# Batch 1's attention in 256-token blocks behind w2, and a re-ordered down projection, in a fused retention and mixer kernel

## The chip, the cores and the metric

The kernel runs on one core of one Trainium2 chip. The metric is the device time of one execution in microseconds, and the median over several runs is what counts. A core has five engines, each with its own in-order instruction queue: TensorE (PE; PEld is its weight load) multiplies matrices into PSUM banks, VectorE (DVE) and ScalarE (ACT) read those banks and write SBUF, GpSimd (POOL) works on SBUF alone, and SyncE (SP) issues transfers. ACT's queue issues transfers too.

## The reference, cut to what matters

Inputs q, k and v have the shape [4 batches, 8 heads, 768 tokens, 64]. The first half is a retention layer, the second a mixer with a low-rank mix over tokens and an MLP over channels:

```
for t in range(S):
    state = gamma * state + outer(k[t], v[t])      # per batch and head
    y[t] = (q[t] @ state) / sqrt(64)
x = y as [4, 768, 512]
u = x + (x^T @ U @ V)^T                            # U: 768 x 32, V: 32 x 768
out = u + relu(u @ w_ch1) @ w_ch2                  # 512 x 2048 and 2048 x 512
```

## The kernel before, in words

**The retention** is computed in pieces of tokens. Powers of gamma are multiplied into q and k when they are cast to bf16. For each piece, scores `a` are the product of k and q, masked (VectorE, L355 or L435); the output is `a` times v plus q times the running state (TensorE, L372/379 or L445/450), copied from PSUM to `xs[b]` by ScalarE; and the state is added up in one PSUM bank over the whole batch (L328 or L415) and copied out by ScalarE.

Batch 0 goes in three blocks of 256 tokens (`prep_block`, `turn_block`, `state_half`, `score_block`, `mix_block`). A partition of a block holds two successive tokens, so a load reads 512 bytes in a row. A block's score has two halves, each of 16 matmuls on a 64x64 part of the array. Batches 1 to 3 go in six chunks of 128 tokens, one token a partition, loads of 256 bytes in a row (`prep_chunk`, `turn_pe` or `turn_dma`, `state`, `score`, `mix`). q and k are needed transposed: batch 1 does that on TensorE (`turn_pe`, through PSUM bank 6 named "qk", evacuated by ScalarE), batches 2 and 3 by DMA transposes on ScalarE's queue.

**The low-rank mix** of a batch: `lr_proj` (L468), `lr_expand` (L478 and the adds at L482), and a transpose of the result into `uT`, by `lr_turn_pe` or by DMA (`lr_turn`).

**The MLP** has an up projection, 32 pieces (16 of 512 tokens, 16 of 256 tokens; four matmuls each, L624), whose ReLU goes to VectorE for each third piece (L629) and to ScalarE for the others (L631). Batch 0's down projection is 24 pieces of four matmuls (L659). The down projections of batches 1 to 3 use Strassen's scheme in Winograd's form: seven products p1 to p7 of half-size blocks for each of three pairs of token tiles, 21 pieces of eight matmuls (`down_pairs`, L552). It needs sums of blocks of w2 (`w2_sums`, 16 VectorE operations in four calls, made once) and of the hidden layer (`g_sums`, four calls of four VectorE operations in each batch). Products gather in PSUM banks named A, B and C; `keep` (L565) and `give` (L571) read them on VectorE.

**The order.** `weave` writes out all queues by hand: the MLP's pieces of batch b-1 in order, and between them the steps of batch b's attention and low-rank mix, each at a mark that is a share of the stage's summed piece costs (a full up piece counts 0.864, a down piece 0.864 or 0.874). A step is put before the first piece that begins at or after its mark.

**Loads.** One list, `feed`, holds all loads in order; SP issues them. Sixteen are issued ahead, and each `take` of a loaded tile issues one more, since a tile's buffer has to be read before it is filled again. The order is batch 0, U and V, w1, one chunk of batch 1 (`AHEAD`), w2, the rest of batch 1, U again in another layout, batches 2 and 3. GpSimd casts nearly everything that is loaded, in the order of the list. The rows of `out` are stored when both halves of a row are ready: batch 0 by SP, in two halves for its interleaved token order, batches 1 to 3 by ScalarE's queue.

**PSUM** has eight banks, given out in rings by `RINGS` (L68): "mlp" has banks 0 to 2, "s" 3 and 4, "o" 5, "qk" 6, "st" 7, A takes 0 and 6 in turn, B 1, C 2.

Of the kernel before, what the change touches and what calls it, by code (L numbers as in the profile page):

```python
# [18 lines left out]
def kernel(  # L19
# [26 lines left out]
    AHEAD = 1  # L46
# [22 lines left out]
             "A": [0, 6], "B": [1], "C": [2]}  # L69
# [42 lines left out]
    def feed_block(sc):  # L112
        for nm, src in (("k", k), ("q", q), ("v", v)):
            for hh in range(2):
                feed.append(((nm, 0, sc, hh),
                             src[0, ds(4 * hh, 4), ts(sc, SC), :].rearrange(
                                 "h (p two) d -> p h (two d)", two=2)))
# [30 lines left out]
    for sc in range(NSC):  # L148
        feed_block(sc)
# [4 lines left out]
    for ci in range(AHEAD):  # L154
        feed_chunk(1, ci)
    for m in range(NM):
        feed.append((("w2", m), moe_w_ch2[ts(m, P)]))
    for b in range(1, B):
        for ci in range(NCK):
            if b > 1 or ci >= AHEAD:  # L160
                feed_chunk(b, ci)
        if b == 1:
            feed.append((("u2",), None))
# [71 lines left out]
    def prep_block(eng, nm, sc, hh):  # L235
        if hh == 0:
            pre[nm, sc] = blk.tile([P, 2, H, D], bf16, tag=nm + "0",
                                name=f"{nm}0_{sc}")
        t = pre[nm, sc][:, :, ds(4 * hh, 4)]
        src = take(nm, 0, sc, hh).rearrange("p (h two d) -> p two h d", h=4,  # L240
# [57 lines left out]
    def turn_block(nm, sc, eng):  # L298
        src = pre[nm, sc]
        tp = bank("mlp", bf16)  # L300
        t = blk.tile([P, 4, 2, P], bf16, tag=nm + "T0",
                      name=f"{nm}T0_{sc}")
# [12 lines left out]
        live[nm, sc] = t  # L315

    def state_half(sc, x):

        kd, vb = pre["k", sc], pre["v", sc]
        first = sc == 0 and x == 0  # L320
        if first:
            live["st_p"] = bank("st")
            live["st", 0, 0] = None
# [13 lines left out]
        live["st", sc + x, 1 - x] = ns  # L337

    def score_block(sc, par, tag="s", engs="DD"):
        kT, qT = live["k", sc], live["q", sc]  # L340
# [9 lines left out]
        for i in range(2):  # L350
            a = blk.tile([P, 4, P], bf16, tag=f"a0{i}{par}",
                          name=f"a0{i}{par}_{sc}")
# [8 lines left out]
            live["a", sc, par, i] = a  # L361

    def mix_block(sc, engs):
        if sc == 0:
            xs[0] = xp.tile([P, NCK, DM], fp16, tag="x", name="x_0")
        qT, vb = live.pop(("q", sc)), pre["v", sc]
        o_p = [bank("o"), bank("qk")]
        for x in range(2):
            st = live.pop(("st", sc, x))
            if st is not None:  # L370
                for p in range(4):
                    nc.tensor.matmul(o_p[x][:, ts(p, P)], qT[:, p, x], st[:, p],  # L372
                                     start=(p == 0), stop=False,
                                     skip_group_check=True)
        for par in range(2):
            for h in range(H):
                for x in range(2):
# [3 lines left out]
                        live["a", sc, par, h % 2][r, h // 2], vb[r, par, h],  # L381
                        start=(sc == 0 and x == 0 and par == 0 and h == 0),
                        stop=True, skip_group_check=True)
        for x in range(2):
            evac(engs[x], xs[0][:, 2 * sc + x], o_p[x])

    def turn_pe(b, ci, eng="A"):
        qkd, vb = pre[b, ci]  # L390
        tp = bank("qk", bf16)
        qkT = rmid.tile([P, 8, P], bf16, tag="qkT", name=f"qkT_{b}_{ci}")
        for i in range(2):
            for p in range(4):
                nc.tensor.transpose(tp[:, ts(4 * i + p, P)],
                                    qkd[:, i, ds(2 * p, 2)], ident)
        evac(eng, qkT, tp.rearrange("p (n m) -> p n m", n=8))
        live[b, ci] = [vb, qkT]

    def turn_dma(b, ci):  # L400
        qkd, vb = pre[b, ci]
        qkT = rmid.tile([P, 8, P], bf16, tag="qkT", name=f"qkT_{b}_{ci}")
        nc.scalar.dma_start_transpose(
# [22 lines left out]
    def score(b, ci):  # L426
# [6 lines left out]
        for i in range(2):  # L433
            a = rmid.tile([P, 4, P], bf16, tag=f"a{i}", name=f"a{i}_{b}_{ci}")
# [29 lines left out]
    def lr_proj(b):  # L464
        p_p = bank("o")
        for j in range(NCK):
            for c in range(NCB):
                nc.tensor.matmul(p_p[ds(RK * c, RK), :P], Ub[b > 0][:, j],  # L468
# [5 lines left out]
    def lr_expand(b, j0, nj, last="qk"):  # L474
        banks = [bank(t) for t in ("s", "s", "o", last)]
        for j in range(j0, j0 + nj):
            for c in range(NCB):
                nc.tensor.matmul(banks[c][:, ts(j - j0, P)],  # L478
                                 V4[b > 0][ds(RK * c, RK), ts(j, P)],
# [6 lines left out]
    def lr_turn_pe(b, j0):  # L486
        tp = bank("qk", fp16)
# [7 lines left out]
    def lr_turn(b, j):  # L495
        nc.scalar.dma_start_transpose(
# [11 lines left out]
    def store():  # L508
        if stores:
            eng, dst, src = stores.pop(0)  # L510
            eng.dma_start(out=dst, in_=src)

# [16 lines left out]
    def g_sums(gT, gS, m):  # L529
# [5 lines left out]
        nc.vector.tensor_tensor(s1, a21, a22, op=ALU.add)  # L535
        nc.vector.tensor_tensor(s2, s1, a11, op=ALU.subtract)
        nc.vector.tensor_tensor(a21, a11, a21, op=ALU.subtract)
        nc.vector.tensor_tensor(s4, a12, s2, op=ALU.subtract)

    def down_pairs(b, gT, gS):  # L540
# [21 lines left out]
        def keep(key, i, nm, j, h):  # L562
            t = outp.tile([P, DQ], fp32, tag=f"d{nm}", bufs=1,
# [5 lines left out]
        def give(key, i, j, h, more):  # L569
# [4 lines left out]
            if r[1] == 2:  # L574
                stores.append((nc.scalar, out[b, ts(j, P)], r[0]))
# [12 lines left out]

        def p5(i):
            product("C", i, s1, t1, True)  # L590

        def p7(i):
            product("A", i, s3, t3, False)
            keep("A", i, "c", i + NP, 1)
            give("C", i, i + NP, 1, held["c", i])
# [9 lines left out]
        order = []  # L605
        for i in range(NP):
            order += [(p1, i)] if i == 0 else []
            order += [(p2, i), (p6, i), (p5, i), (p7, i)]
            order += [(p1, i + 1)] if i + 1 < NP else []
            order += [(p4, i), (p3, i)]  # L610
        return [(0.874, part(f, i)) for f, i in order]

    def mlp_pieces(b):
# [4 lines left out]
        def up(m, lo, sz):  # L618
            j, nj = lo // P, sz // P

            def f():
# [6 lines left out]
                if n[0] % 3 == 0:  # L628
# [10 lines left out]
        else:  # L639
            def both(t, i):  # L640
                return [t[i], t[i + 1], t[i + NH], t[i + NH + 1]]

            pieces += both(lo, 0) + both(lo, 2) + both(hi, 0)
            pieces += both(hi, 2) + both(lo, 4) + both(hi, 4)
            pieces += both(lo, 6) + both(hi, 6)
            gS = gtp.tile([P, 3, NH, TH], fp16, tag="gS", name=f"gS_{b}")
            for i, at in ((0, 15), (2, 19), (4, 26), (6, len(pieces) - 1)):
                cost, f = pieces[at]
                pieces[at] = (cost, chain(f, part(g_sums, gT, gS, i)))
            return pieces + down_pairs(b, gT, gS)  # L650
        hold = {}

        def down(j, m0):
            def f():
# [6 lines left out]
                if m0 == NM - 4:  # L661
# [3 lines left out]
                    dst = out[b, ts(j, P)]  # L665
                    if b:
                        stores.append((nc.scalar, dst, o_sb))
                    else:
                        for i in range(2):
                            stores.append((nc.sync, dst.rearrange(  # L670
                                "(p two) c -> two p c", two=2)[i],
                                o_sb[ds(HP * i, HP)]))
# [37 lines left out]
    def prep_pair(nm, sc, engs):  # L710
        for hh in range(2):
            prep_block(engs[hh], nm, sc, hh)
# [3 lines left out]
    for sc in range(NSC):  # L716
        last = sc + 1 == NSC
        keep_busy(3 if sc else 9, fresh=True)
        turn_block("k", sc, "D")
        keep_busy(0 if sc else 7)  # L720
        turn_block("q", sc, "AD" if last else "A")
        prep_pair("v", sc, "PA")
        if sc:
            state_half(sc - 1, 1)
            mix_block(sc - 1, "AA")
        else:
            keep_busy(4)
        score_block(sc, 0)
        if not last:
            prep_pair("k", sc + 1, "PD")  # L730
            keep_busy(3)
            score_block(sc, 1)
            prep_pair("q", sc + 1, "PD")
            keep_busy(1)
        else:
            score_block(sc, 1, "mlp", "DA")
        state_half(sc, 0)
# [5 lines left out]
    mix_block(NSC - 1, "AD")  # L743
# [20 lines left out]

    for ci in range(AHEAD):
        prep_chunk(1, ci)
    for j in range(4):
        prep_w2(j)
    for b in range(1, B + 1):
        tracks = []  # L770
        if b > 1:
            first = [part(lr_expand, b - 1, 4, 2),
                     part(lr_turn_pe if b == 2 else lr_turn, b - 1, 4)]
        tracks.append((first, 0.02, 0.2 if b == 1 else 0.06))
        if b < B:
            if b == 1:
                at = [0.5, 0.6, 0.655, 0.715, 0.77, 0.825]
                lag = [0.01, 0.035, 0.065]
                turn = turn_pe
                for i in range(AHEAD, NCK):  # L780
# [54 lines left out]
```

## Time and profile before

| | us |
|---|---|
| median of 13 runs | 247.17 (244.94 to 249.11) |
| the profiled execution's own time | 245.95 |
| its span, from the first to the last instruction | 244.1 |
| TensorE busy | 217.5 |
| VectorE busy | 145.8 |
| ScalarE busy | 87.5 |
| GpSimd busy | 83.9 |

A few groups of instructions from the page's table. The columns are the line, the engine, the operation, what is written from what, the tiles and the count; then the busy time and the mean nanoseconds of one; then the idle time of the engine just before, and what ended it:

```profile
L624 PE MATMUL mlp<-uT,w1b 128*128 128x512 f16 (+1 forms) x512 | 89.3, 326 | 3.4 <-ACT gT L631 1.3
...
L435 DVE TENSOR_TENSOR a<-s,mask 128x512 bf16<-128x512 f32 x36 | 23.0, 680 | 7.5 <-PE s L431 7.5
...
L552 PE MATMUL A<-w2t,gS 128*128 128x256 f16 x72 | 9.3, 272 | 4.1 <-DVE da L565 4.1
```

The up projection is the largest group. TensorE sat idle for little of the time before any one group; a wait for VectorE's `da` is the largest of the down products. The duration that a timeline row shows for a group of matmuls ends after the next group has begun, because matmuls are pipelined; the step from start to start is what a group costs the queue.

### The profile page before, as it was taken

How to read it: one execution, taken by the hardware profiler on the slowest of the kernel's cores; microseconds unless marked ns; L12 is line 12 of the kernel's file. 1: busy time of each engine (PE TensorE's matmuls, PEld its weight loads, DVE VectorE, ACT ScalarE, POOL GpSimd, SP SyncE). 2: the span in 40 equal slices, each digit the busy share in tenths (PEclk: the TensorE clock that was granted, in tenths of full speed). 3: DMA queues.
4: the chain of work that ended last, by engine and by line, in shares of the span. 5: the costliest groups of instructions: out<-in, count | busy, mean ns of one | idle time of the engine just before them, and what ended most of it. 6: DMA issues, size and time to landing. Idle time of an engine off the chain costs nothing. (4 is left out here: it accounts for less than half of the span.)

```text
span 244.1 us, 5336 instructions
## 1 busy us (share of the span) xinstructions
PE 217.5 (89%) x2152; PEld 143.9 (59%) x2152; DVE 145.8 (60%) x289; ACT 87.5 (36%) x175; POOL 83.9 (34%) x121
## 2 busy tenths in 40 slices
PE   7898999999999589877679979999799889998993
PEld 3466544866555245543578753765688645656882
DVE  6577445338796632786575663496855652856442
ACT  3267354554643154554320002665221014541000
POOL 5542988687888481366425100000000000000000
PEclk9999999999999999999999999999999999999999
DMA  6998999999999998999993155322222352000222
GB/s 182 295 290 211 298 343 272 383 238 212 224 212 217 232 233 193 227 192 230 206 202 110 66 107 148 70 47 43 43 53 82 109 149 46 0 0 4 86 86 89
DMA packets 94633, 39.22 MB, mean 161 GB/s; under 512 B 78096, under 2 KB 87312, under 8 KB 94608
## 3 DMA queue, kind: packets, MB, share of 16 engines
q1 hardware_dynamic: 73008, 29.43, 51.9%
q10 hardware_dynamic: 21600, 9.44, 17.0%
q8 instruction: 17, 0.28, 0.5%
q14 instruction: 8, 0.07, 0.1%
HBM read 27.85 MB, written 6.29 MB: 140 GB/s over the span
## 5 line engine op out<-in xcount | busy, mean ns | idle before, releaser
L624 PE MATMUL mlp<-uT,w1b 128*128 128x512 f16 (+1 forms) x512 | 89.3, 326 | 3.4 <-ACT gT L631 1.3
L624 PEld LDWEIGHTS <-w1b 128*128 128x128 f16 x512 | 48.1, 98 | 35.7 <-issue 4.6
L631 ACT ACTIVATE gT<-mlp 128x512 f16<-128x512 f32 (+1 forms) x88 | 43.2, 498 | 62.9 <-PE mlp L624 39.7
L629 DVE TENSOR_SCALAR gT<-mlp 128x256 f16<-128x256 f32 (+1 forms) x40 | 21.4, 535 | 36.4 <-PE mlp L624 36.3
L552 PEld LDWEIGHTS <-gT 128*128 128x128 f16 x288 | 27.4, 98 | 8.0 <-issue 4.6
L435 DVE TENSOR_TENSOR a<-s,mask 128x512 bf16<-128x512 f32 x36 | 23.0, 680 | 7.5 <-PE s L431 7.5
L84 ACT ACTIVATE x<-o 128x512 f16<-128x512 f32 x21 | 12.5, 596 | 37.0 <-PE o L450 23.9
L552 PEld LDWEIGHTS <-gS 128*128 128x128 f16 x216 | 20.7, 98 | 7.2 <-issue 4.4
L659 PE MATMUL mlp<-w2b,gT 128*128 128x512 f16 x96 | 24.2, 380 | 0.0
L263 POOL TENSOR_TENSOR qkd<-in,gq 128x512 bf16<-128x512 f32 x18 | 19.4, 1076 | 10.7 <-DMA in<-in_q_dram 9.0
L263 POOL TENSOR_TENSOR qkd<-in,gk 128x512 bf16<-128x512 f32 x18 | 20.0, 1110 | 8.5 <-DMA in<-in_k_dram 8.3
L552 PE MATMUL A<-w2t,gT 128*128 128x256 f16 x144 | 18.6, 272 | 3.0 <-DVE dc L565 1.5
L84 ACT ACTIVATE state<-st 64x256 bf16<-64x256 f32 x40 | 15.0, 375 | 7.0 <-PE st L328 3.8
L261 POOL CAST vd<-in 128x512 bf16<-128x512 f32 x18 | 11.8, 654 | 15.8 <-issue 9.6
L552 PE MATMUL A<-w2t,gS 128*128 128x256 f16 x72 | 9.3, 272 | 4.1 <-DVE da L565 4.1
L450 PE MATMUL o<-vd,a 128*128 128x64 bf16 x144 | 8.0, 194 | 5.2 <-DVE a L435 5.0
L659 PEld LDWEIGHTS <-gT 128*128 128x128 f16 x96 | 8.2, 98 | 7.2
L177 PE MATMUL mlp<-ones 128*128 128x512 bf16 x34 | 10.9, 451 | 1.4 <-DVE ones L170 1.4
L482 DVE TENSOR_TENSOR x<-s,x 128x256 f16<-128x256 f32 (+1 forms) x16 | 8.2, 552 | 5.8 <-PE qk L478 4.7
L565 DVE TENSOR_TENSOR dc<-A,x 128x256 f32<-128x256 f32 x9 | 3.8, 424 | 11.9 <-PE A L552 11.9
L290 POOL CAST w2b<-in 128x512 f16<-128x512 f32 x16 | 9.8, 616 | 3.1 <-DMA in<-in_moe_w_ch_dram 2.4
L450 PEld LDWEIGHTS <-a 128*128 128x128 bf16 x144 | 6.2, 98 | 6.9 <-DVE a L435 6.4
(110 smaller groups left out, 271.8 us busy)
## 6 DMA issues: line engine op xcount, KB each, us to landing
in<-in_moe_w_ch_dram SPq DMA_DIRECT2D x32, 256.0 KB, 5.9
in<-in_k_dram SPq DMA_DIRECT2D x24, 256.0 KB, 5.2
in<-in_q_dram SPq DMA_DIRECT2D x24, 256.0 KB, 5.5
in<-in_v_dram SPq DMA_DIRECT2D x24, 256.0 KB, 5.4
out_dram<-o ACTq DMA_DIRECT2D x18, 256.0 KB, 2.0
out_dram<-o SPq DMA_DIRECT2D x12, 128.0 KB, 3.6
Vf<-in_moe_V_dram SPq DMA_DIRECT2D x4, 96.0 KB, 3.6
qkT<-qkd ACTq DMA_TRANSPOSE x12, 3.3
```

The costliest lines, as they stand in the source:

```text
L84: nc.scalar.activation(dst, src, AF.Copy)
L177: nc.tensor.matmul(idle_bank[0], ones[:, :P], ones, start=True, stop=True, skip_group_check=True)
L261: nc.gpsimd.tensor_copy(out=t, in_=src)
L263: nc.gpsimd.tensor_tensor(t, src, g[:, ci, :, None].to_broadcast([P, H, D]), op=ALU.mult)
L290: nc.gpsimd.tensor_copy(out=w2b[:, m], in_=take("w2", m))
L435: nc.vector.tensor_tensor(a, four(sp[i]), causal(mask), op=ALU.mult)
L450: nc.tensor.matmul(o_p[:, ts(h, D)], a[i][:, h // 2], vb[:, h], start=(ci == 0 and h == 0), stop=True, skip_group_check=True)
L552: nc.tensor.matmul(acc[key, i], lhs[:, m, ts(i, P)], rhs[:, m], start=(fresh and m == 0), stop=(m == NH - 1), skip_group_check=True)
L624: nc.tensor.matmul(g_p[:, :sz], w1b[:, c, ts(m, P)], uTs[b][:, ds(j, nj), c], start=(c == 0), stop=(c == NCB - 1))
L629: nc.vector.tensor_relu(gT[:, m, ds(lo, sz)], g_p[:, :sz])
L631: nc.scalar.activation(gT[:, m, ds(lo, sz)], g_p[:, :sz], AF.Relu)
L659: nc.tensor.matmul(ch, gT[:, m, ts(j, P)], w2b[:, m], start=(m == 0), stop=(m == NM - 1))
```

## The change

1. **Batch 1 in blocks.** It takes batch 0's path: three blocks, two tokens a partition, 512-byte loads. All its casts are on GpSimd. The k transpose is evacuated by ScalarE, the q transpose by VectorE; both use the "qk" bank, as does the second output of `mix_block`. Its token order is then interleaved, so it uses the first layout of U and V (`Ub[b > 1]`), and its rows of `out` are stored in two halves, on ScalarE's queue (`keep_row`).
2. **Its place.** No chunk of batch 1 is loaded ahead of w2 any more. The marks of its steps and of `w2_sums` are new.
3. **Down projection.** The 21 products come in a written-out order in which the A chains of pairs 0 and 1 interleave (two A banks, the first one 6); `give` of C's first result (`c22`) happens when both p5 and p7 are done; the `keep` tiles get two buffers.
4. **Spread sums.** The four operations of a `g_sums` call follow four successive pieces, one each; the last call's are put behind the last up piece (two) and the first two down pieces.
5. **Smaller edits.** From batch 1's MLP on, each fourth ReLU instead of each third goes to VectorE, and the "mlp" ring has four banks (6, 0, 1, 2). `lr_turn_pe` of batch 1's last part uses the "o" bank, `lr_expand` of the last tiles "st". The score tiles `a0` and `a1` have two buffers instead of four. Stores of batches 2 and 3 and the DMA transposes of batch 3 go to SP's queue.

The diff's core:

```diff
-    AHEAD = 1
-             "A": [0, 6], "B": [1], "C": [2]}
+             "A": [6, 0], "B": [1], "C": [2]}
...
-    for ci in range(AHEAD):
-        feed_chunk(1, ci)
     for m in range(NM):
         feed.append((("w2", m), moe_w_ch2[ts(m, P)]))
-    for b in range(1, B):
+    for sc in range(NSC):
+        feed_block(1, sc)
+    feed.append((("u2",), None))
+    for b in range(2, B):
         for ci in range(NCK):
-            if b > 1 or ci >= AHEAD:
-                feed_chunk(b, ci)
-        if b == 1:
-            feed.append((("u2",), None))
+            feed_chunk(b, ci)
...
+            pool, tag = (rpre, "qkd") if b else (blk, nm + "0")
...
+        tp = bank("qk" if b else "mlp", bf16)
...
-        nc.scalar.dma_start_transpose(
+        (nc.sync if b > 2 else nc.scalar).dma_start_transpose(
...
+            a = rmid.tile([P, 4, P], bf16, tag=f"a{i}", bufs=2,
...
+    def keep_row(b, j, row):
+        dst = out[b, ts(j, P)]
+        if b > 1:
+            stores.append((nc.sync, dst, row))
+            return
+        for i in range(2):
+            stores.append((nc.scalar if b else nc.sync, dst.rearrange(
+                "(p two) c -> two p c", two=2)[i], row[ds(HP * i, HP)]))
...
+        def c22(i, nm):
+            done.add((nm, i))
+            if ("p5", i) in done and ("p7", i) in done:
+                give("C", i, i + NP, 1, held["c", i])
...
-        order = []
-        for i in range(NP):
-            order += [(p1, i)] if i == 0 else []
-            order += [(p2, i), (p6, i), (p5, i), (p7, i)]
-            order += [(p1, i + 1)] if i + 1 < NP else []
-            order += [(p4, i), (p3, i)]
+        order = [(p1, 0), (p1, 1), (p2, 0), (p6, 0), (p6, 1), (p5, 0), (p7, 0),
+                 (p7, 1), (p2, 1), (p4, 0), (p3, 0), (p4, 1), (p5, 1), (p1, 2),
+                 (p2, 2), (p6, 2), (p3, 1), (p7, 2), (p5, 2), (p4, 2), (p3, 2)]
...
-                if n[0] % 3 == 0:
+                if n[0] % (3 if b == 0 else 4) == 0:
...
-            for i, at in ((0, 15), (2, 19), (4, 26), (6, len(pieces) - 1)):
-                cost, f = pieces[at]
-                pieces[at] = (cost, chain(f, part(g_sums, gT, gS, i)))
-            return pieces + down_pairs(b, gT, gS)
+            late(pieces, 12, g_sums(gT, gS, 0))
+            late(pieces, 16, g_sums(gT, gS, 2))
+            late(pieces, 24, g_sums(gT, gS, 4))
+            s1, s2, s3, s4 = g_sums(gT, gS, 6)
+            late(pieces, len(pieces) - 1, [chain(s1, s2)])
+            down = down_pairs(b, gT, gS)
+            late(down, 0, [s3, s4])
+            return pieces + down
...
-            first = [part(lr_expand, b - 1, 4, 2),
-                     part(lr_turn_pe if b == 2 else lr_turn, b - 1, 4)]
+            first = [part(lr_expand, b - 1, 4, 2, "st"),
+                     part(lr_turn_pe, 1, 4, "o") if b == 2 else
+                     part(lr_turn, b - 1, 4)]
+            if b == 2:
+                RINGS["mlp"] = [6, 0, 1, 2]
...
-                at = [0.5, 0.6, 0.655, 0.715, 0.77, 0.825]
-                lag = [0.01, 0.035, 0.065]
+                at = [0.46, 0.57, 0.68]
+                lag = [0, 0, 0.12]
+                for i in range(NSC):
+                    for nm, d in (("k", 0), ("q", 0.005), ("v", 0.01)):
+                        tracks.append((
+                            [part(prep_block, "P", nm, 1, i, hh)
+                             for hh in range(2)], at[i] - 0.1 + d, at[i] - 0.1 + d))
+                    for f, d in ((part(turn_block, "k", 1, i, "A"), 0),
+                                 (part(turn_block, "q", 1, i, "D"), 0.022),
+                                 (part(state_half, 1, i, 0), 0.03),
+                                 (part(score_block, 1, i, 0), 0.046),
+                                 (part(score_block, 1, i, 1), 0.07),
+                                 (part(mix_block, 1, i, "AA"), lag[2])):
+                        tracks.append(([f], at[i] + d, at[i] + d))
+                    if i + 1 < NSC:
+                        tracks.append(([part(state_half, 1, i, 1)],
+                                       at[i] + 0.085, at[i] + 0.085))
...
-                    tracks.append(([part(w2_sums, m)], 0.58 + 0.05 * m, 1))
+                    tracks.append(([part(w2_sums, m)], 0.46 + 0.025 * m, 1))
```

## The prediction

> **What bounds the kernel now.** I read the page's busy row first, then TensorE's waits, then the timelines of TensorE, VectorE and GpSimd around each gap.
>
> ```profile
> PE 217.5 (89%) x2152; PEld 143.9 (59%) x2152; DVE 145.8 (60%) x289; ACT 87.5 (36%) x175; POOL 83.9 (34%) x121
> ```
>
> TensorE (PE) is busy 217.5 of 244.1 us and runs one hand-ordered queue to the last product, so time is won or lost where that queue has work or waits. The clock row is 9 (full) in all slices. TensorE's timeline gives the stages: batch 0's attention to 28.6 us; batch 0's MLP with batch 1's attention woven in, 28.6 to 87.4 (stage 1); MLP 1 with batch 2's attention to 146.6 (stage 2); MLP 2 with batch 3's to 198.0 (stage 3); MLP 3 alone to the end (stage 4). What TensorE waited for:
>
> ```profile
> PE o L450 <- DVE a L435: 5.0, 7, 2.6
> PE A L552 <- DVE da L565: 4.1, 3, 2.0
> PE A L552 <- DVE dc L565: 1.5, 3, 0.5
> PE A L552 <- DVE db L565: 1.5, 2, 0.9
> ...
> PE qk L490 <- DVE x L482: 1.4, 2, 0.8
> ...
> PE s L478 <- DVE pc L86: 1.2, 1, 1.2
> PE qk L490 <- ACT uT L84: 1.1, 1, 1.1
> ```
>
> Nearly all are VectorE (DVE) late with a small tile behind a row of sums, none a load. By stage the timeline's gaps add to 4.0 us (stage 1 from 49.4 on), 10.0 (stage 2), 3.7 (stage 3), 2.2 (stage 4). The largest in stages 2 to 4:
>
> ```profile
> 108.03 0.29 PE L450 MATMUL o<-vd,a 128*128 128x64 bf16 x4 [1.01 <-DVE a L435]
> ...
> 116.90 0.29 PE L450 MATMUL o<-vd,a 128*128 128x64 bf16 x4 [2.58 <-DVE a L435]
> ...
> 123.39 1.03 PE L552 MATMUL A<-w2t,gS 128*128 128x256 f16 x8 [2.00 <-DVE da L565]
> ...
> 146.62 1.02 PE L624 MATMUL mlp<-uT,w1b 128*128 128x512 f16 x4 [0.54 <-DVE o L571]
> ```
>
> **Part 1: spread sums, new order of the down products, fourth MLP bank.** The p6-after-p1 gaps (2.00, 1.41, 0.65) arise because four sums of 0.55 us stand before `da`; now `da` stands behind two, and two products lie between: gone. The p4-after-p7 gaps (0.51 in each stage) get a product in between. The waits for a bank or evacuation (0.83, 0.50, 0.24, 0.47) go with four MLP banks and a free first A bank. But part of the gaps at the ends of stages 2 and 3 won't return. There the low-rank expansion starts at 138.55, its four adds end at 141.9, two DMA transposes are issued at 141.98 and 143.3, and a transpose takes 3.2 us to land: 146.5, just when the first product of MLP 2 starts. The new order leaves the same six products (5.2 us) after the expansion, so 0.94+0.51+0.54 in stage 2 and 0.57+0.51+0.53 in stage 3 stay as a wait for `uT`.
>
> Stage 4 gains 0.24+0.47+0.65+0.51 = 1.9; stage 3 gains 0.50+0.15+1.41 = 2.1. In stage 2 the 0.83, the 2.00 and the `a` waits (1.01+0.31+2.58+0.31) are open, 7.0 together; but VectorE still does 16 sums, now one per piece. At four half-size pieces of 0.44 us each with a sum of 0.57 (0.73 with GpSimd beside it) it falls behind, and masks queue there: I work out about 1 to 2.2 us left before the second `mix` and 1.1 to 1.7 before the fourth. Gain 3.0 to 6.0, taken 4.3. Sum of part 1: -8.3.
>
> **Part 2: batch 1 in blocks: TensorE's work.** From batch 0's rows (start to start): a state half 0.55 (8 products), a score half 0.35 (16), a block's mix 0.57, four state products 0.22, a block transpose 0.45. New: 5x0.55 + 6x0.35 + 3x0.57 + 5x0.22 = 7.7. Old: 5x0.22 + 6x0.33 + 6x0.23 + 5x0.22 = 5.6. Transposes: 48 either way. So +2.1, on the path, since TensorE hardly waits there. Evacuations are equal in number; three of six transposed tiles move from ACT to DVE (0.68 as batch 0's kT).
>
> **Part 3: batch 1 loaded behind w2.** GpSimd's casts show when loads came:
>
> ```profile
> 36.65 0.62 POOL L284 CAST w1b<-in 128x512 f16<-128x512 f32 x1 [0.22 <-DMA in<-in_moe_w_ch_dram]
> ...
> 52.67 0.62 POOL L290 CAST w2b<-in 128x512 f16<-128x512 f32 x1 [0.16 <-DMA in<-in_moe_w_ch_dram]
> 53.59 1.04 POOL L263 TENSOR_TENSOR qkd<-in,gq 128x512 bf16<-128x512 f32 x1 [0.31 <-DMA in<-in_q_dram]
> ```
>
> w1's last block landed at 36.6, w2's at 52.6, with three 256-byte-run loads between. Without those, w2's sixteen loads at 0.67 us (w1's best) to 0.82 end at 47.4 to 49.7. Then k's halves land 0.9 apart, as batch 0's, and cost GpSimd 1.04 each, then q's, then v's 0.61: k ready at 50.5 to 52.7, q 2.1 later, v 1.3 after that. TensorE reaches the first transpose (mark 0.46, before the 14th half-size piece) at 49.4; today's first chunk was prepared at 40. Wait 1.0 to 4.5 over k, q and v; taken 2.9. SP's later loads are queued behind the same ring as before; nothing else waits.
>
> [...]
>
> **Part 4: batch 1's chain of waits.** Blocks share bank 6 ("qk") between transposes and the second mix output; each next user waits for ScalarE (1.02 a transpose, 1.1 two x tiles). Walking the marks piece by piece (0.87 a full piece), waits appear: score half 2 behind the masks 0.6; first mix behind kT's evacuation 1.25; second q transpose 0.4; second mix 0.2; third q transpose, put right behind that mix, 1.25; projection behind two evacuations 0.4; the uT transpose one piece after the expansion instead of two, with its adds done 3.0 after it, 1.8, then 0.35. That is 6.25 without the w2 sums.
>
> The w2 sums move from every 0.1 of the stage to every 0.05, from mark 0.46. Their price now:
>
> ```profile
> 56.69 0.42 DVE L527 TENSOR_TENSOR w2t<-w2b,w2t 128x512 f16<-128x512 f16 x1
> 57.04 1.26 DVE L527 TENSOR_TENSOR w2t<-w2b 128x512 f16<-128x512 f16 x1
> 58.22 1.26 DVE L527 TENSOR_TENSOR w2t<-w2b,w2t 128x512 f16<-128x512 f16 x1
> ```
>
> [...] I take the row: four at 3.1 us. Queued behind them are the masks and qT; with `a` of two masks at 1.28, the second block's scores wait 0.75 and 1.85: 2.6 more. Waits of stage 1: 2.9+6.25+2.6 = 11.75 in place of 4.0, so +7.75; with the work, +9.85.
>
> **Small edits.** Twelve half-row stores on ScalarE's queue replace six (0.34 us an issue, 2 us more in stage 2's down part, where ACT is busy 3.15 of 20); stores and transposes of batch 3 go to SP, whose loads are issued by 125 us. Behind them wait only x evacuations with a piece or more of slack: nothing, or up to 0.5 either way if one is caught. Two `a` buffers instead of four: a mask waits for the mix two chunks back, earlier in the order: nothing, at most 0.3. One ReLU in four on VectorE is in part 1.
>
> **Sum.** -8.3 + 9.85 = +1.55 on the profiled execution (245.95 us: span 244.1 and 1.85 around it): 247.5. The median of 13 runs, 247.17, lies 1.2 above that run: 248.7.
>
> **Rivals.** *The later stages win* (not slower): batch 1 comes in time (1.0 instead of 2.9) and GpSimd is idle during the w2 sums, since it waits for `rpre` buffers until batch 1's tiles are read, so 2.6 vanishes: stage 1 +5.35, and stage 2 yields 6.0: total -4.65, 242.5; halfway, at -2.3, 244.9. For it: GpSimd's idle rows after 93 us, made by such buffers. Against: it is 80% busy from 54 to 79. It decides once stage 1 loses less than the 8.3 that the later stages win. [...] *It cancels*: losses and gains within 1.2. *The new order doesn't free TensorE* because every product still meets a VectorE result: part 1 yields only the 2.0 of bank waits, +7.8, 255; its chance is in the second's.
>
> **Numbers.** A difference below about 0.5% (1.2 us) can't be told from none here. Slight loss as summed 0.42, its own range 246.5 to 251.5; later stages win 0.36 (242.5 to 245.9); lock 0.09; cancels 0.13. About a fifth of the first lies inside 0.5%. Faster 0.37, same 0.20, slower 0.43. Range 242.0 to 252.5, the rivals' full strength left out at both ends.
>
> **What would show it.** Right: MLP 1 starts near 97 instead of 87.4; first block transpose waits for GpSimd's k; bank-6 waits on ScalarE; no `da` or `dc` wait left; `uT` waits of about 2 us before MLP 2 and 3; stage 4 1.9 shorter. Wrong: MLP 1 before 94, or w2 sums at 0.41, or stage 2 shorter by 6.

## The result, and the profile after

The changed kernel took 249.91 us (median of 11 runs, 248.32 to 250.54; one more run on record, not counted in it, took 247.51), against 247.33 for the kernel before, whose runs now number 48 (244.94 to 249.11). The ratio is 1.0103 (95% interval 1.0081 to 1.0126): slower by 1%. Its profiled execution took 249.7 us with a span of 247.9, so 3.8 more of span than before. Here and below a ratio leaves out the runs more than 1.5% above the fastest of their kernel; medians and ranges keep them.

Stages are counted as in the prediction, from the first up product of one MLP to that of the next:

| us | start | stage 1 | stage 2 | stage 3 | stage 4 |
|---|---|---|---|---|---|
| before | 28.6 | 58.8 | 59.2 | 51.4 | 46.1 |
| after | 28.8 | 73.3 | 53.8 | 48.8 | 43.2 |
| change measured | +0.2 | +14.5 | -5.4 | -2.5 | -2.9 |
| change forecast | | +9.85 | -4.3 | -2.1 | -1.9 |

The later stages won 10.8 us and stage 1 lost 14.5. First the page of the changed kernel: TensorE's busy row, and the row of the clock granted to it, in tenths, one digit for each 6.2 us.

```profile
PE 222.6 (90%) x2268; PEld 146.0 (59%) x2268; DVE 149.1 (60%) x286; ACT 86.9 (35%) x178; POOL 84.3 (34%) x121
...
PEclk9999999999986999999999999999999999999998
```

TensorE is busy 5.1 us longer, more than the 2.1 of added work that was forecast. The digits 8 and 6 at 68 to 81 us tell part of why: there the clock was not full. (The last digit, 8, falls behind the last product, which ends at 244.4, and costs nothing.) What TensorE waited for (total, times, longest):

```profile
PE s L344 <- DVE a L357: 4.0, 6, 2.5
PE o L442 <- DVE a L427: 2.5, 4, 1.2
...
PE qk L303 <- POOL k L247: 1.8, 2, 1.0
PE qk L482 <- DVE x L474: 1.7, 1, 1.7
...
PE qk L303 <- ACT x L83: 1.4, 2, 1.2
```

The waits for `da` and `dc` are gone. In their place stand batch 1's block steps: score behind a mask, block transpose behind GpSimd's k, and users of bank 6 behind an evacuation. TensorE's timeline has them in their places; a row is a start, a duration and a group of products, and the bracket is the idle time before it and what ended it.

```profile
50.80 0.40 PE L303 MATMUL qk<-ident,k 128*128 128x128 bf16 x4 [1.05 <-POOL k L247]
...
68.48 0.42 PE L344 MATMUL s<-qT,kT 64*64 64x128 bf16 x16 [1.13 <-DVE qT L85]
68.83 1.04 PE L674 MATMUL mlp<-w2b,gT 128*128 128x512 f16 x4
72.41 0.32 PE L344 MATMUL s<-qT,kT 64*64 64x128 bf16 x2 [2.54 <-DVE a L357]
...
73.58 1.89 PE L674 MATMUL mlp<-w2b,gT 128*128 128x512 f16 x4
...
82.40 0.61 PE L303 MATMUL qk<-ident,q 128*128 128x128 bf16 x8 [1.17 <-ACT x L83]
```

The longest wait, 2.54, is the second score half of block 2. VectorE's timeline at that place shows what stood ahead of the mask it needed:

```profile
68.35 1.14 DVE L528 TENSOR_TENSOR w2t<-w2b 128x512 f16<-128x512 f16 x1
69.60 1.08 DVE L528 TENSOR_TENSOR w2t<-w2b,w2t 128x512 f16<-128x512 f16 x1
70.60 0.82 DVE L528 TENSOR_TENSOR w2t<-w2b 128x512 f16<-128x512 f16 x1
71.34 0.41 DVE L528 TENSOR_TENSOR w2t<-w2b,w2t 128x512 f16<-128x512 f16 x1
71.68 1.27 DVE L357 TENSOR_TENSOR a<-s,mask 128x512 bf16<-128x512 f32 x2
```

A whole `w2_sums` call, 3.4 us here, runs before the two masks. Right after this wait the same four products of L674 take 1.89 instead of 1.04. The table of stretches (length, busy time and count of each engine, then the granted clock) cuts the place into three of equal length:

```profile
68.93:72.34 3.41, 0.94 (x4) 0.31 (x4) 3.31 (x6) 0.00 (x0) 2.21 (x3) 1.00 1.26 219
72.34:75.75 3.41, 3.06 (x24) 1.31 (x24) 2.15 (x5) 0.00 (x0) 0.00 (x0) 0.50 1.30 222
75.75:79.17 3.42, 3.42 (x20) 2.01 (x18) 0.44 (x1) 0.76 (x2) 2.60 (x3) 0.50 0.98 214
```

After a stretch of 3.41 us in which TensorE was busy 0.94, the clock was 0.50 for 6.83 us. Of those it was busy 6.48. If that work takes half as long at a clock of 1.00, as the 1.04 against 1.89 nearly has it, the cost is an estimated 3.2 us.

**Theory:** stage 1's loss of 14.5 is 7.4 of waits (TensorE is idle 11.4 after and 4.0 before), 3.2 of clock, and 3.9 of further busy time. Of the last, 2.1 was forecast as added work; experiment 3 measures it. The part that can be undone is the place of the w2 sums: it makes the 2.5 us wait and, through it, the half clock. **Rivals:** the late loads of batch 1 set the loss (then moving block 0 ahead of w2 mends it); the sums only pass their wait on to the next user of VectorE (then moving them gives nothing); part 1 and the blocks disturb one another (then the parts don't add).

### The profile page after: what moved, and what is told of

Its sections match the earlier page's. It is cut to its first block, busy times and chain, and to the rows that moved or that the text cites. A ratio compares the mean times of both kernels' runs of the same rounds, so it can differ in the third digit from the quotient of the medians.

```text
span 247.9 us, 5585 instructions
## 1 busy us (share of the span) xinstructions
PE 222.6 (90%) x2268; PEld 146.0 (59%) x2268; DVE 149.1 (60%) x286; ACT 86.9 (35%) x178; POOL 84.3 (34%) x121
## 4 chain that ended last, share of the span: by engine, by line
PE 59%; DVE 18%; DMA 12%; POOL 3%; issue 3%; ACT 1%; SPq 1%; ACTq 1%; DVEq 0%
PE mlp L629 22%; PE A L552 10%; PE mlp L674 6%; DMA in<-in_moe_w_ch_dram 5%; DVE w2t L528 4%; PE C L552 4%; DVE x L474 3%; DVE a L357 3%; PE B L552 3%; DVE gS L496 3%; DMA uT<-x 3%; DMA in<-in_k_dram 2%; DMA in<-in_q_dram 2%; DVE a L427 2%; PE st L326 2%
## 5 line engine op out<-in xcount | busy, mean ns | idle before, releaser
L636 ACT ACTIVATE gT<-mlp 128x512 f16<-128x512 f32 (+1 forms) x94 | 45.5, 490 | 60.4 <-PE mlp L629 45.7
L634 DVE TENSOR_SCALAR gT<-mlp 128x512 f16<-128x512 f32 (+1 forms) x34 | 18.9, 555 | 32.2 <-PE mlp L629 32.0
L674 PE MATMUL mlp<-w2b,gT 128*128 128x512 f16 x96 | 25.6, 403 | 0.0
L83 ACT ACTIVATE x<-o 128x512 f16<-128x512 f32 x18 | 10.7, 597 | 34.7 <-PE o L442 22.3
L261 POOL TENSOR_TENSOR qkd<-in,gk 128x512 bf16<-128x512 f32 x12 | 13.3, 1110 | 16.2 <-DMA in<-in_k_dram 16.2
L261 POOL TENSOR_TENSOR qkd<-in,gq 128x512 bf16<-128x512 f32 x12 | 13.3, 1109 | 15.0 <-PE st L326 5.4
L357 DVE TENSOR_TENSOR a<-s,mask 128x512 bf16<-128x512 f32 x22 | 14.1, 682 | 7.1 <-PE s L344 7.1
L427 DVE TENSOR_TENSOR a<-s,mask 128x512 bf16<-128x512 f32 x24 | 15.4, 682 | 1.9 <-PE s L422 1.7
L674 PEld LDWEIGHTS <-gT 128*128 128x128 f16 x96 | 8.4, 101 | 9.2 <-issue 1.7
L259 POOL CAST vd<-in 128x512 bf16<-128x512 f32 x12 | 7.8, 654 | 13.7 <-issue 13.0
L247 POOL TENSOR_TENSOR q<-in,gq 128x512 bf16<-128x512 f32 x9 | 10.0, 1129 | 3.5 <-DMA in<-in_q_dram 3.5
L344 PE MATMUL s<-qT,kT 64*64 64x128 bf16 x176 | 6.1, 229 | 5.4 <-DVE a L357 4.0
L247 POOL TENSOR_TENSOR k<-in,gk 128x512 bf16<-128x512 f32 x9 | 9.8, 1101 | 3.0 <-DMA in<-in_k_dram 3.0
```

The lines of the kernel that those rows point to most:

```text
L83: nc.scalar.activation(dst, src, AF.Copy)
L247: (nc.gpsimd if eng == "P" else nc.vector).tensor_tensor(t, src, g.to_broadcast([P, 2, 4, D]), op=ALU.mult)
L261: nc.gpsimd.tensor_tensor(t, src, g[:, ci, :, None].to_broadcast([P, H, D]), op=ALU.mult)
L357: nc.vector.tensor_tensor(a, four(sp[i]), m, op=ALU.mult)
L427: nc.vector.tensor_tensor(a, four(sp[i]), causal(mask), op=ALU.mult)
L634: nc.vector.tensor_relu(gT[:, m, ds(lo, sz)], g_p[:, :sz])
```

## The experiments

Ratios are to runs of the kernel before that were taken beside each experiment; their medians are 247.6 for experiments 1 to 4, 246.92 for 5 to 8 and 247.61 for 9 to 12.

**1. Part 1 alone.** Before, with the new down order, spread sums, four MLP banks, the ReLU share, and the smaller edits; batch 1 stays in chunks, ahead of w2.

```diff
+        order = [(p1, 0), (p1, 1), (p2, 0), (p6, 0), (p6, 1), (p5, 0), (p7, 0),
...
+            late(pieces, 12, g_sums(gT, gS, 0))
...
-        nc.scalar.dma_start_transpose(
+        (nc.sync if b > 2 else nc.scalar).dma_start_transpose(
```

> The kernel before with part 1 alone (order of the down products, spread sums, fourth MLP bank, one ReLU in four on VectorE, stores and batch 3's transposes on SP, two a buffers); batch 1 stays in chunks ahead of w2. My theory: stage 1 stays at the 58.8 us from 28.6 to 87.4, and stages 2 to 4 shorten as in the changed kernel (5.4 + 2.5 + 3.0 = 10.9 us by its TensorE timeline), so about 236.5 against 247.3. Rival, that part of the later gain comes from batch 1's earlier loads and shorter DMA: less than 8 us gained, above 239.5. Rival, that part 1 frees nothing by itself: 247.

Measured: 239.52 (239.16 to 240.62), ratio 0.9677 (0.9611 to 0.9743); 8.1 faster, but 3 short of the 236.5 expected. Stages 58 / 57.0 / 50.4 / 43.1: stage 2 won too little. At its end TensorE's timeline has a wait that the changed kernel doesn't have, and a slow product behind it:

```profile
143.97 1.42 PE L629 MATMUL mlp<-uT,w1b 128*128 128x512 f16 x4 [3.77 <-DMA uT<-x]
```

The last add for `uT` ended on VectorE at 136.16. ScalarE's and SyncE's queues at that place, in the same kernel:

```profile
139.40 2.64 ACTq L497 DMA_TRANSPOSE uT<-x  x2
```

```profile
127.31 9.53 SPq L403 DMA_TRANSPOSE qkT<-qkd  x4
```

ScalarE issued `uT`'s first transpose 3.2 us after its data were ready. SyncE, which ran far ahead, had issued batch 3's first four transposes until 136.8; the last of these landed at 139.30. ScalarE's queue waits on the semaphores of the second, third and fourth of them one by one, at 136.69, 138.50 and 139.32, each just after its landing. So the program, as built, makes the transposes of the two queues wait for one another. In the changed kernel, whose order is the same, batch 3's landed at 150.33, before the adds ended (151.2): hidden there. After the wait the clock was again half for 3.41 us.

**2. The blocks alone.** The changed kernel with part 1 undone (only the two `a` buffers stay): the other half of the same diff.

```diff
-        order = [(p1, 0), (p1, 1), (p2, 0), (p6, 0), (p6, 1), (p5, 0), (p7, 0),
...
+            order += [(p2, i), (p6, i), (p5, i), (p7, i)]
...
-            late(pieces, 12, g_sums(gT, gS, 0))
...
+            for i, at in ((0, 15), (2, 19), (4, 26), (6, len(pieces) - 1)):
```

> The changed kernel with part 1 undone: batch 1 in blocks behind w2 and the early w2 sums, but the old down order, sums in rows, three MLP banks, stores and transposes on ScalarE's queue. Theory: stage 1 as long as in the changed kernel (73.5 us instead of 58.8), later stages as in the kernel before: 247.3 + 14.7 = 262. Rival, that the parts disturb each other (stage 1 is made long by the new order of queues): under 257.

Measured: 259.57 (257.52 to 261.68), ratio 1.0452 (1.0358 to 1.0545), 2.4 less than expected. Stage 1 is 73.1, as in the changed kernel, and stages 2 to 4 (59.3, 51.5, 45.7) are those of before. The two halves, -8.1 and +12.0, sum to +3.9; together they gave +2.6. They nearly add, within the intervals of the ratios (1.6 and 2.3 us either way), so the rival that they disturb one another falls, but for experiment 1's transposes.

**3. The w2 sums later.** The four calls start at mark 0.58 and stand 0.1 apart, as before's did.

```diff
-                    tracks.append(([part(w2_sums, m)], 0.46 + 0.025 * m, 1))
+                    tracks.append(([part(w2_sums, m)], 0.58 + 0.05 * m, 1))
```

> The changed kernel with one edit: the w2 sums go back to the marks of the kernel before (0.58, 0.68, 0.78, 0.88). Theory: the waits of 1.1 and 2.5 us of the second block's scores and the 6.8 us at half clock after them vanish (3.7 + 3.4 us), while a sum or two now meets the low-rank tail (up to 1.5 us back): 243 to 245 against 249.9, mean clock above 0.995. Rival, that the waits come from bank 6 and ScalarE and not from VectorE's queue: under 2 us gained. Rival, the clock falls by the load of the stage and not by that wait: clock stays 0.985.

Measured: 242.49 (241.86 to 243.48), ratio 0.9793 (0.9726 to 0.9861); 7.4 less than the changed kernel, more than expected. The stretch of stage 1 (kernel before, changed kernel, then this one; columns as above):

```profile
28.62:87.40 58.78, 54.78 (x498) 31.25 (x497) 35.48 (x59) 26.91 (x48) 45.09 (x59) 1.00 1.05 260
```

```profile
28.81:102.11 73.30, 61.88 (x613) 34.12 (x612) 39.76 (x61) 23.98 (x45) 50.10 (x65) 0.95 0.92 232
```

```profile
28.93:94.45 65.52, 58.83 (x613) 32.67 (x612) 37.12 (x61) 23.96 (x45) 48.98 (x65) 1.00 0.99 260
```

The same 613 products take 3.05 us less at full clock, and TensorE is idle 4.7 less (73.30 - 61.88 against 65.52 - 58.83). VectorE's 61 operations are 2.6 shorter; of the w2 sums' two forms, eight each, the median went from 0.94 to 0.98 (`w2t<-w2b`) and from 1.08 to 0.43 (`w2t<-w2b,w2t`). Against the kernel before, both at full clock, these products keep TensorE busy 4.0 us longer (58.83 against 54.78): that is the added work of the blocks, where 2.1 was forecast. In TensorE's waits in the whole kernel, the score's is down from 4.0:

```profile
PE s L344 <- DVE a L357: 1.4, 5, 0.4
```

One line was thus worth 7.4 us: 4.7 of idle and 3.05 of clock in stage 1, where 3.2 was estimated. The wait was not passed on, so that rival falls.

**4. The long wait filled.** Ten products of ones, read by nobody and no part of the computation, ahead of block 2's second score half: TensorE waits as long, but isn't idle.

```diff
+    def score_busy(i):
+        keep_busy(10, fresh=True)
+        score_block(1, i, 1)
...
-                                 (part(score_block, 1, i, 1), 0.07),
+                                 (part(score_busy, i) if i == 1 else
+                                  part(score_block, 1, i, 1), 0.07),
```

> The changed kernel with ten idle products of 512 columns (2.2 us at full clock, not part of the computation) put in TensorE's queue right ahead of the second score half of the second block, where TensorE waits 2.5 us; nothing else. The wait itself stays (the masks come no earlier), only TensorE is busy in it. Theory, that the idle time lowers the clock: no half clock, about 3 us gained, 246.5 to 247.5. Rival, that the clock drop is unrelated to the idle time or costs nothing: 249.9 and a mean clock of 0.985.

Measured: 247.78 (246.4 to 250.66, 20 runs), ratio 1.0012 (0.9986 to 1.0038); 2.1 less than the changed kernel. The ten runs with a mean clock of 0.997 or more have a median of 247.0, the six at or below 0.986 one of 249.2. The profiled one is of the second kind; its TensorE timeline shows that the filled place kept its clock and that another wait lost it:

```profile
52.90 0.40 PE L303 MATMUL qk<-ident,k 128*128 128x128 bf16 x4 [2.77 <-POOL k L247]
...
54.48 1.92 PE L633 MATMUL mlp<-uT,w1b 128*128 128x256 f16 x8
...
72.17 2.32 PE L174 MATMUL mlp<-ones 128*128 128x512 bf16 x10
...
75.76 1.04 PE L678 MATMUL mlp<-w2b,gT 128*128 128x512 f16 x4
```

The products after the filler take 1.04, at full clock; those after the wait for k take 1.92, where eight of this shape take 1.04 in the changed kernel at 52.21. The half clock is therefore a price of the idle, separable from the wait, of about 2 to 3 us (249.9 against 247.8, and against the 247.0 at the higher clocks).

**5. Part 1 without its transposes on SyncE.** Experiment 1 with batch 3's transposes back on ScalarE's queue.

```diff
-        (nc.sync if b > 2 else nc.scalar).dma_start_transpose(
+        nc.scalar.dma_start_transpose(
```

> Part 1 alone as in the first experiment, but batch 3's DMA transposes stay on ScalarE's queue (stores of batches 2 and 3 stay on SP). In the first experiment TensorE waited 3.8 us for uT before MLP 2: its transposes, ready to start at 136.2, were issued at 139.4, right after the fourth of batch 3's transposes, which SP had run ahead, had landed (139.3); a half clock of 3.4 us followed. Theory: the uT transposes wait for SP's transposes; on one queue this order can't arise, the wait falls to 0.6 and the half clock goes: 3.1 + 1.6 less, 235 against 239.5. Rival, that uT is late by the DMA queues' load: 239 to 240.

Measured: 236.1 (234.67 to 238.92), ratio 0.9559 (0.9446 to 0.9671). That is 3.4 less than experiment 1, or 2.9 by the ratios, whose intervals overlap; the trace is clearer. `uT`'s wait before MLP 2 is 0.65 instead of 3.77 and no clock is lost there; that before MLP 3 grew from 0.62 to 1.47. Two runs at full clock took 234.7; those at 0.997 and 0.991 took 237.5 and 238.9. The one at 0.997 is the profiled one, and its half clock begins at 234.41, behind the last product, so the 2.8 us that it lost are not the clock's; they stay unexplained.

**6 and 7. Each half of part 1's down projection undone.** From experiment 5: the sums in rows of four again, or the old order again.

```diff
-            late(pieces, 12, g_sums(gT, gS, 0))
...
+            for i, at in ((0, 15), (2, 19), (4, 26), (6, len(pieces) - 1)):
+                late(pieces, at, [chain(*g_sums(gT, gS, i))])
```

```diff
-        order = [(p1, 0), (p1, 1), (p2, 0), (p6, 0), (p6, 1), (p5, 0), (p7, 0),
...
+            order += [(p2, i), (p6, i), (p5, i), (p7, i)]
```

> The kernel of e5 with one part undone: the four sums of each call stand in a row again, at the places of the kernel before; the new down order stays. Theory (the da waits of 2.00, 1.41 and 0.65 come from the row before da): but in the new order two products lie between da and its reader, so the rows cost only what they exceed those by, 0.3 a stage, and the a waits of stage 2 grow by 1 to 2: 1.5 to 3 us slower than e5. Rival, that spreading is what frees TensorE: 4 us or more. Rival, that it does nothing: within 0.7.

> The kernel of e5 with the old order of the 21 down products; sums stay spread. Theory: p4 right behind p7 costs 0.5 a stage, but in stages 2 and 3 the wait for uT swallows it; da behind two sums with one product in between costs 0.3 to 0.6 a stage: 1 to 2.5 us slower than e5. Rival, that the order is what frees TensorE: 4 us or more.

Measured: 240.05 (239.13 to 241.04), ratio 0.9739 (0.9663 to 0.9815), and 241.54 (238.94 to 241.93), ratio 0.9764 (0.9654 to 0.9873). Both cost 4 to 5.4, as the rivals of the two expectations had it, where less was expected. The one run of each at full clock, 239.13 and 238.94, stands 4.4 and 4.3 above those of experiment 5. Rows bring back an `a` wait of 2.76 before batch 2's `mix`, and `da` waits up to 1.02; the old order brings back `da` (1.04 in stage 2) and `dc` (0.52 a stage):

```profile
PE A L552 <- DVE da L565: 2.4, 3, 1.0
PE A L552 <- DVE dc L565: 1.5, 3, 0.5
```

So each half is worth about 4.4 where the other is in place; twice that fits within part 1's 10.8 (experiment 5), and what one is worth without the other was not run. Both profiles have two stretches of 3.41 us at half clock: one behind waits at the end of stage 1, which neither edit touches, and one in stage 2 behind the wait for `a` before batch 2's `mix` (2.76 with rows, 1.75 with the old order, 1.48 in experiment 5).

**8. Block 0 of batch 1 ahead of w2**, in the changed kernel: the loads' place taken by itself.

```diff
+    feed_block(1, 0)
     for m in range(NM):
         feed.append((("w2", m), moe_w_ch2[ts(m, P)]))
-    for sc in range(NSC):
+    for sc in range(1, NSC):
...
+    for nm in "kqv":
+        for hh in range(2):
+            prep_block("P", nm, 1, 0, hh)
```

> The changed kernel with one edit: the first block of batch 1 is loaded and cast ahead of w2. Theory: the waits of the first block for k and q (1.05 + 0.78 + 0.24 + 0.47 us) vanish and w2, 5 us later, is still in time for the down products or a little late; the waits on VectorE and bank 6 and the half clock stay: 247 to 248 against 249.9. Rival, that the load order sets the whole chain of stage 1 (an early start keeps it ahead of everything): under 244. Rival, that w2's lateness takes it all back: 249.5 or more.

Measured: 249.89 (247.94 to 250.95), ratio 1.0129 (1.0034 to 1.0223): nothing gained in the median. The waits for k and q, 2.5 us, are gone; the second block's waits for VectorE grew from 1.13 and 2.54 to 1.63 and 2.94, and the half clock stayed. TensorE came 1.7 us earlier to a row of sums that ended 1.3 earlier. The rival that loads set the loss falls, since under 244 was asked of it, and no wait of TensorE or VectorE names w2, so w2's later arrival isn't seen to cost anything. Yet the move is not worth nothing in every run: the profiled one, the fastest, with 6.83 us at half clock like the changed kernel's, has stage 1 at 70.95, 2.35 shorter. Two of the other three, at clocks of 0.972 and 0.973, took 250.95 and 250.58.

**9 and 10. Two further edits on experiment 3:** block transposes in the MLP's banks instead of bank 6 (9, shown), and experiment 8's move (10).

```diff
-        tp = bank("qk" if b else "mlp", bf16)
+        tp = bank("mlp", bf16)
```

> The kernel of e3 (changed kernel, w2 sums at the old marks) with batch 1's block transposes in the mlp ring's banks instead of bank 6. Theory: the waits behind ScalarE in bank 6 (1.11 before the first mix, 1.17 before the third q transpose, 0.2 between) vanish: 2.3 less than e3, 240 to 240.5. Rival, that the mix then waits for its masks or x tiles anyway: within 1 of e3.

> The kernel of e3 with the first block of batch 1 loaded and cast ahead of w2, as in e8. In e8 the 2.5 us of waits for k and q vanished from the trace, yet the second block's waits for VectorE grew from 3.7 to 4.6 us. Theory: behind that stood VectorE's w2 sums; with these moved away, the early block pays: 1.5 to 2.3 less than e3, 240.2 to 241. Rival, that w2 coming 5 us later costs as much, or that TensorE meets another wait next: within 0.8 of e3.

Measured: 242.06 (240.54 to 243.71), ratio 0.9775 (0.9712 to 0.9839), and 240.15 (239.77 to 241.02), ratio 0.9709 (0.9681 to 0.9737). Experiment 9 took away the two waits for bank 6 (1.11 and 1.17), but its profile waited for k (2.13 and 0.60), and 3.41 us ran at half clock: no gain, and undecided. Experiment 10 gained 2.3 on experiment 3, as expected: the same move that gained nothing in the median with the sums early pays once VectorE is not late. (Experiment 3's own profile waits 1.1 for k; stage 1 is 1.9 shorter in experiment 10's.)

**11. The block version with everything mended:** experiments 10 and 9 together, batch 3's transposes on ScalarE, and batch 1's `uT` transposes about one piece later.

```diff
-        tp = bank("qk" if b else "mlp", bf16)
+        tp = bank("mlp", bf16)
...
-                               t + 0.07, t + 0.09))
+                               t + 0.085, t + 0.125))
```

> Batch 1 in blocks with every wait of stage 1 mended that the runs showed: w2 sums at the old marks, block transposes in mlp banks, first block ahead of w2, the two uT transposes later (two pieces behind the expansion, and one apart), batch 3's transposes on ScalarE. Theory: e3's stage 1 of 65.5 us loses 2.3 + 2.0 + 0.9 = 5.2, to 60.3, later stages as in the changed kernel: 237 to 238, still 1 to 2 behind batch 1 in chunks with the same part 1 (e5, 236.1), by the 2.1 us of extra TensorE work. Rival, that blocks win once mended: under 235.5. Rival, that the waits only move: above 240.

Measured: 238.22 (236.96 to 240.76), ratio 0.9609 (0.9571 to 0.9648). Stage 1 is still 62.5, against 59.2 in chunks in experiment 5. The profiled run is the slowest of the four, and 3.41 us of its stage 1 ran at half clock, an estimated 1.7 of the 3.3. By the ratios the blocks stand 0.5% behind experiment 5, with intervals that overlap: no run shows that blocks reach the chunks, and that they fall short of them is not clear of the noise.

**12. Chunks kept busy.** Experiment 5 with twelve products of ones, again no part of the computation, in the three waits at the end of stage 1.

```diff
+                       ([chain(part(keep_busy, 5, True), part(lr_expand, b, 0, 4, "qk"))
...
+                tracks.append(([chain(part(keep_busy, 3), part(lr_turn_pe, b, 0)),
+                                 chain(part(keep_busy, 4), part(lr_turn_pe, b, 2))],
```

> The kernel of e5 with twelve idle products (not part of the computation, 2.6 us at full clock) put into the three waits at the end of stage 1 (1.35 before the expansion, 0.78 and 1.11 before the uT transposes); nothing else. Theory: the half clock of 3.4 us that some runs have (mean clock 0.991 to 0.993 against 1.0, 2 to 4 us longer) comes from idle windows such as this one; fewer runs have it, so the median falls by 0.5 to 1.5 from 236.1 to about 235, and the fastest run stays at 234.7. Rival, that the idle products delay the work behind them: above 236.5.

Measured: 236.4 (235.6 to 236.97), ratio 0.9551 (0.9522 to 0.9579). The expected gain did not come: the ratio is experiment 5's within noise, and the fastest run is 0.9 higher. But all four runs had the full clock, and they spread over 1.4 instead of 4.3. With four runs each, and one of experiment 5's slower ones not slowed by its clock, that the spread shrank by the filler isn't shown. These two are the best versions found, about 4.5% faster than before.

## Why the prediction came out as it did

The time was forecast at 248.7 and came at 249.9, by two errors that partly offset, so that its nearness is in part luck: stage 1 lost 4.65 more than forecast, the later stages won 2.5 more. The 4.65 are the clock (3.1, forecast at nothing) and the added work (4.0 for 2.1), less 0.35 of waits.

**The step that failed: "The clock row is 9 (full) in all slices."** It was read as given. The chain of waits forecast in part 4 makes an idle of 2.5 us, and no term prices what the clock does after it: 3.2 us, or 3.05 by experiment 3. The changed kernel's trace has the clock at 0.50 for 6.83 us, right behind a stretch of 3.41 us in which TensorE was busy 0.94. The profile of before held no sign of it: there the clock is 1.00 up to the last product.

**The chain of waits in stage 1** was right in place and nearly in size: 11.4 against 11.75. The measured rows below are from TensorE's timeline.

| wait | forecast | measured |
|---|---|---|
| first block's k, q, v | 2.9 | 2.5 |
| score half 2 behind the masks, first and third block | 0.6 | 0.5 |
| first mix behind kT's evacuation | 1.25 | 1.1 |
| second q transpose | 0.4 | 0.2 |
| second block's scores behind the w2 sums | 2.6 | 4.0 |
| third q transpose | 1.25 | 1.2 |
| second mix, projection | 0.6 | none |
| uT transposes | 2.15 | 1.9 |

The mis-sized wait is that for the w2 sums: calls of 4.1, 3.9, 3.7 and 3.4 us (from start to end). The forecast's "row" is that of these sums before, here in its two forms; their mean is 0.81, and 3.1 a call was taken from it:

```profile
L527 DVE TENSOR_TENSOR w2t<-w2b,w2t 128x512 f16<-128x512 f16 x8 | 6.7, 840 | 0.4
...
L527 DVE TENSOR_TENSOR w2t<-w2b 128x512 f16<-128x512 f16 x8 | 6.2, 777 | 0.0
```

Single ones took 0.41 to 1.26 in both kernels: 0.41 or 0.42 where GpSimd was busy beside them for 0.29 us or less, 0.56 to 1.26 where for 0.55 or more. It was busy in 11.1 of their 12.9 us before and in 14.4 of the 15.3 after.

**The added work** was forecast at 2.1 and is 4.0 by experiment 3. From start to start there, with idle time left out, the block's state, score and mix products take 9.1 (2.9, 2.8 and 3.35), where the forecast had 7.7, against 6.1 for the chunks', where it had 5.6. A score half took 0.47 instead of 0.35, because its second half is split by a wait. The rest is about 0.6 in the transposes and 0.5 in the MLP's own products, which are interrupted more often.

**Part 1** was forecast at -8.3. Stage by stage -5.4, -2.5 and -2.9 against -4.3, -2.1 and -1.9. The waits that should go went; of the `a` waits, 1.25 + 0.31 remained at the second `mix` and 0.61 + 0.31 at the fourth (forecast 1 to 2.2 and 1.1 to 1.7). The tails stayed as forecast, as 1.11 for `db` and 0.6 for `uT` in stages 2 and 3. Stage 4 has no wait left: 2.2 were there, of which the forecast kept 0.3. The 0.7 beyond the waits is busy time: the same 304 products took 39.6 instead of 40.4. By experiments 6 and 7 either the spread or the order undone gives back about 4.4.

**Load order.** What the 512-byte loads are worth isn't shown: no wait of TensorE's in stage 1 names a load, but its waits for k stand behind GpSimd's casts and those behind k's loads, and no run changes the size of the loads alone. By experiments 8 and 10 what mattered was when k is there, 2.5 us, and only if VectorE is in time. That k came at 50 to 53 us in different kernels of the same load order isn't explained.

**Stores and transposes of batch 3 on SP** were put at "nothing, or up to 0.5". In the changed kernel this held; with part 1 alone it cost about 3 (experiments 1 and 5). The slow stage 1 is not what hid it: in experiments 3 and 10, with stage 1 at 65.5 and 63.6, `uT`'s wait is 0.7 as well. Why batch 3's transposes stand clear of `uT`'s with the blocks and not with the chunks stays open.

**The rivals.** *The later stages win* had the later stages right (-10.8 against -4.3, -2.1 and -1.9 with stage 2 at up to -6.0) and stage 1 wrong; it decides at a stage-1 loss under what the later stages win, and 14.5 is over 10.8. Moved sums (experiment 3) put stage 1 at +6.7 and the total on its side. What the 0.09 of *lock* rests on, no run shows; measured were w2 calls of 3.4 to 4.1 us and waits for k, q and v of 2.5. *It cancels* took a difference within 1.2; measured were 2.6. *The new order doesn't free TensorE*, whose chance lies in those 0.09, falls with experiments 1 and 5.

The profiles differ by 3.8 of span (forecast 1.55) and the medians by 2.6. Before's profiled run had the full clock, while nearly all of its other runs stood at 0.993 or less, which is 3.41 us or more at half clock. That before pays a part of this price too, unseen in its profile, would explain the difference; but while its runs at 0.985 and 0.986 took 248.3 to 249.6, one at 1.000 took 247.43, as long as those at 0.993, so it stays a guess.

## What to carry to other kernels

Take a change of several parts apart before judging it: here one part was worth -3.2% as it stood (-4.4% mended) and the other +4.5%, and the sum was a loss of 1%. Price an idle stretch of the matrix engine with the clock after it: idle of about 2 us within 3.41 cost an estimated 1.7 to 3.2 us more, in some runs and not in others. Place long rows of work on a shared engine by what queues behind them; one line that moved four rows of sums was worth 7.4 us, and until it was moved, an earlier load gained nothing in the median.

## What the hardware showed that was not expected

- Ahead of the last product, every stretch below full clock in the profiles was at 0.50 and lasted 3.41 or 6.83 us. Within each profile the changes of the clock lie whole multiples of 3.413 us apart: in the changed kernel the drop comes at 72.34, the return two such windows later at 79.17, the next drop 49 later at 246.42 (174.08 us from drop to drop, 51 windows). With the windows known from this, TensorE's busy time in each can be read. In the 14 profiles, 11 full-clock windows ahead of the last product had it busy 1.51 us or less (0.49 to 1.51), and half clock followed every one. Of all the others there, busy 1.60 or more, one was followed by half clock (1.89, experiment 11; not explained). So what counted here was busy time in a fixed window, not one long idle: nearly the same waits at the end of stage 1 left 1.71 us of a window busy in experiment 5 and 1.51 in experiment 6, and only experiment 6 lost its clock. The pairs of rows are the window and the one behind it, in experiment 5 and then in 6.

```profile
84.22:87.63 3.41, 1.71 (x20) 1.23 (x20) 0.54 (x1) 1.48 (x2) 2.38 (x3) 1.00 0.85 188
87.63:91.05 3.42, 2.90 (x21) 1.05 (x19) 2.11 (x5) 1.71 (x3) 1.95 (x2) 1.00 1.26 232
```

```profile
82.87:86.28 3.41, 1.51 (x17) 0.99 (x16) 1.31 (x3) 1.02 (x1) 1.50 (x2) 1.00 0.98 233
86.28:89.70 3.42, 3.42 (x14) 1.28 (x10) 0.69 (x1) 1.02 (x1) 2.60 (x3) 0.50 0.98 219
```

- A transpose DMA on ScalarE's queue was held for 3.2 us until transposes from SyncE's queue had landed, though neither reads what the other writes. It was held by semaphore waits that the built program has, so this run doesn't show what the hardware would do without them.
